# Banded attention and two MoE layers on one core: a new order of ScalarE's and VectorE's work in each attention step

## The chip, the cores and the metric

The kernel runs on one core of a Trainium2 chip. The metric is device time in microseconds (us) of one launch, the median over runs: 1203.46 us before the change (three runs, 1202.03 to 1204.03).

## What is computed

Attention with 4 batches, 8 heads, 768 positions and 64 channels, with a causal band of 96 positions and 8 global columns, then two feed-forward blocks over the 3072 tokens, all in float32:

```python
scores = scale * np.matmul(q, k.transpose(0, 1, 3, 2)) + bias     # bias: -slope * distance
scores = np.where(keep, scores, -1000000000.0)
scores = scores - np.max(scores, axis=-1, keepdims=True)
a = np.exp(scores)
a = a / (np.sum(a, axis=-1, keepdims=True) + 1e-09)
x = np.matmul(a, v)                       # 4 x 8 x 768 x 64, turned into 3072 x 512
h = x @ w_in                              # 512 -> 2048
x = (h * np.clip(h + 3.0, 0.0, 6.0) / 6.0) @ w_out
out = ((x @ w1) * (x @ w2) @ w3) @ w_out2 # 512 -> 1024 -> 1024 -> 512
```

## The kernel before

**Split products.** Most matrix products are made from two parts of each operand: a high part, which ScalarE rounds from the value, and a low part, the value minus the high part, which VectorE or GpSimd subtracts. `split_ps` (L353 to L364) does this for a tile in PSUM: ScalarE's copy (L357) makes the high part `...h`, and the closure `low` makes the low part `...l` on VectorE (L360). With a list as `later` the closure is only appended, and its instruction is issued where the list is run. `mm3` (L66) issues the three products high-high, low-high, high-low.

**Units and steps.** Attention is cut into 32 units (batch, half of the positions, pair of heads) of three steps each; a step `s` is one block of 128 queries for two heads. The loop at L608 is a software pipeline written by hand; each engine works through its instructions in the order in which this loop issues them:

- Every second step (a pair step) TensorE computes the products with v of two earlier steps (`a_pv`, tile `pv`, one PSUM buffer), then the scores of two new steps (`a_scores`, tiles `s0`, `s1`).
- In the first step of a unit `prep_k` transposes the next unit's k (`pk`), in the second `prep_q` its q (`pq`). ScalarE makes `kh` (three copies) or `qh`. From unit 8 on the scores take split operands, and the low parts `kl` (three, L360) or `ql` (L392) go to the list `lows`. Units below 8 have no low parts here (ScalarE's copy is then L355).
- `a_trans` transposes the weights of two steps ago (`pt`), `a_copy` brings them to SBUF on ScalarE (`p`, L461). `pk`, `pq` and `pt` share two PSUM buffers.
- `a_norm` makes the reciprocal of the row sums `su` on VectorE (L444, L445) and multiplies `e` by it on GpSimd (L446). `a_max` adds the bias and takes the row maxima on VectorE (L429, two per step), `a_exp` the exponentials on ScalarE (L438).
- `a_out` splits the products with v (`pv`) into `xt0h`/`xt0l` or `xt1h`/`xt1l`, the input of the first feed-forward layer.
- `tick` advances the conversion of the feed-forward weights, which come as float64: ScalarE makes `cva` (L158) from the loaded tile `st`, VectorE joins the bits in `cvt` (L171, L173, L175), ScalarE rounds `wa` (L184), and VectorE (for the first weights) or GpSimd makes its low part (L185). A step has one to four ticks, four while the weights of the first products are awaited (L605).
- `fill.run` puts matmuls of the feed-forward layer of an earlier block (`h`, `x`, L66) with their gates (L513 on ScalarE, L514 on VectorE, L497 and L500 for the parts `g`) between these. The first filler is added after step 14.

In a step VectorE's order before is: the reciprocal, the low parts of the products with v, the maxima, conversions and gates, and the low parts in `lows` after `a_exp`, with two conversions' places ahead of them where there are four ticks. ScalarE's is: `kh` or `qh`, the high parts of the products with v, conversions and gates, `p`, the exponentials.

Of the kernel before, what the change touches and what calls it, by code (L numbers as in the profile page):

```python
# [74 lines left out]
def kernel(ctx: ExitStack, tc: tile.TileContext, q, k, v, n_global, n_local,  # L75
# [104 lines left out]
    def awaited(*kinds):  # L180
        return any(key is not None and key[0] in kinds for key in queued)
# [40 lines left out]
    def tick(n=1):  # L222
        for _ in range(n):
            next(ticks)
            ticked[0] += 1
# [122 lines left out]
    def new_prep(i):  # L348
        def two(tag, shape):
            return tuple(att.tile(shape, F32R, tag=tag + z, name=tag + z) for z in "hl")  # L350
        prep[i] = dict(q=two("q", [P, HB * P]), k=two("k", [P, 2 * HB, P]))

    def split_ps(hi, lo, src, later=None, whole=False):  # L353
        if whole:
            nc.scalar.activation(hi.bitcast(F32), src, AF.Copy)  # L355
            return
        nc.scalar.activation(hi, src, AF.Copy)  # L357

        def low():
            nc.vector.tensor_tensor(lo, src, hi.bitcast(F32), ALU.subtract)  # L360
        if later is None:
            low()
        else:
            later.append(low)  # L364

    def prep_k(i, later):
        hf = units[i][1]
        nk = HB + hf
        kr = raw[i][0].rearrange("p n j d -> p n (j d)")
        ps = psa.tile([P, HB + 1, P], F32, tag="pt", bufs=2, name="pk")  # L370
        for s in range(nk):
            nc.tensor.transpose(ps[:, s, :], kr[:, s, :], ident)  # L372
        own, gp = (0, 1) if hf == 0 else (1, 0)
        ng = HB - 1 + hf
        kh, kl = (x.rearrange("p (n s) c -> p n s c", s=2) for x in prep[i]["k"])
        split_ps(kh[:, :, own], kl[:, :, own], ps[:, hf:hf + HB], later, i < WHOLE)
        split_ps(kh[:, :ng, gp, GW:], kl[:, :ng, gp, GW:], ps[:, 0:ng, GW:], later, i < WHOLE)
        src = ps[:, 0:1, 0:GW].to_broadcast([P, ng, GW])
        split_ps(kh[:, :ng, gp, 0:GW], kl[:, :ng, gp, 0:GW], src, later, i < WHOLE)

    def prep_q(i, later):
        b, hf, hp = units[i]
        qr = raw[i][1].rearrange("p n j d -> p n (j d)")
        ps = psa.tile([P, 512], F32, tag="pt", bufs=2, name="pq")
        for s in range(HB):
            nc.tensor.transpose(ps[:, s * P:(s + 1) * P], qr[:, s, :], ident)
        qh, ql = prep[i]["q"]
        src = ps[:, 0:HB * P]
        sc = qsc[:, hp:hp + 1]
        nc.scalar.activation(qh.bitcast(F32) if i < WHOLE else qh, src, AF.Copy, scale=sc)  # L390
        if i >= WHOLE:
            later.append(lambda: nc.vector.scalar_tensor_tensor(ql, src, sc, qh.bitcast(F32), ALU.mult, ALU.subtract))  # L392
# [4 lines left out]
    def kidx(hf, u):  # L397
        if hf:
            return 2 * u, 2
        return (0, 1) if u == 0 else (2 * u - 1, 2)  # L400

    def a_scores(sts):

        sc = [psa.tile([P, 2, 2 * P], F32, tag=f"s{j}", name=f"s{j}") for j in range(2)]
        for half, st in enumerate(sts):
            i, u = st
            b, hf, hp = units[i]
            c0, nk = kidx(hf, u)
            W = nk * P
            qq, kk = prep[i]["q"], prep[i]["k"]  # L410
            passes = ((0, 0),) if i < WHOLE else ((0, 0), (1, 0), (0, 1))
            for z, (a, b_) in enumerate(passes):
                for j in range(2):
                    r0 = D * j
                    x = qq[a][r0:r0 + D, u * P:(u + 1) * P]
                    y = kk[b_][r0:r0 + D, c0:c0 + nk, :].rearrange("p a c -> p (a c)")
                    if i < WHOLE:
                        x, y = x.bitcast(F32), y.bitcast(F32)
                    nc.tensor.matmul(sc[j][:, half, :W], x, y, start=(z == 0), stop=(z == len(passes) - 1))  # L419
            sm[st] = dict(sc=[x[:, half] for x in sc], W=W, nk=nk, c0=c0, hp=hp)  # L420

    def a_max(st):
        d = sm[st]
        W, hp = d["W"], d["hp"]
        e = att.tile([P, 2, 2 * P], F32, tag="e", name="e", bufs=3)
        mx = att.tile([P, 2], F32, tag="mx", name="mx", bufs=3)
        bs = base0 if d["nk"] == 1 else base1
        for j in range(2):
            nc.vector.tensor_tensor_reduce(e[:, j, :W], d["sc"][j][:, :W], bs, -slope[2 * hp + j], 3.0e38,  # L429
                                           ALU.add, ALU.min, mx[:, j:j + 1])  # L430
        d["e"], d["mx"] = e, mx
# [9 lines left out]
    def a_norm(st):  # L441
        d = sm[st]
        W, su = d["W"], d["su"]
        nc.vector.tensor_scalar(su, su, 1.0e-9, None, ALU.add)  # L444
        nc.vector.reciprocal(su, su)  # L445
        nc.gpsimd.tensor_tensor(d["e"][:, :, :W], d["e"][:, :, :W], su.unsqueeze(2).to_broadcast([P, 2, W]), ALU.mult)  # L446

    def a_trans(st):
        d = sm[st]
        nk = d["nk"]  # L450
        ps = psa.tile([P, 2, 2, P], F32, tag="pt", bufs=2, name="pt")
        for j in range(2):
            for t in range(nk):
                nc.tensor.transpose(ps[:, t, j, :], d["e"][:, j, t * P:(t + 1) * P], ident)  # L454
        d["pt"] = ps

    def a_copy(st):
        d = sm[st]
        nk = d["nk"]
        d["p"] = att.tile([P, 2, 2, P], F32, tag="p", name="p", bufs=4)  # L460
        nc.scalar.activation(d["p"][:, :nk], d["pt"][:, :nk], AF.Copy)  # L461

    def a_pv(sts):

        ps = psa.tile([P, 2, P], F32, tag="pv", name="pv")
        for half, st in enumerate(sts):
            i, u = st
            d = sm[st]
            nk, c0 = d["nk"], d["c0"]
            for t in range(nk):  # L470
                for j in range(2):
                    nc.tensor.matmul(ps[D * j:D * j + D, half], raw[i][2][:, c0 + t, j, :], d["p"][:, t, j, :],  # L472
                                     start=(t == 0), stop=(t == nk - 1))
        sm[sts[0]]["pv"] = ps

    def a_out(sts):
        ps = sm[sts[0]]["pv"]
        runs = [(0, 2)] if sts[0][0] == sts[1][0] else [(0, 1), (1, 2)]
        low = []
        for h0, h1 in runs:  # L480
            i, u = sts[h0]
            b, hf, hp = units[i]
            xh, xl = xT[(2 * b + hf) % 2]
            cs = slice(u * P, (u + h1 - h0) * P)
            split_ps(xh[:, hp, cs], xl[:, hp, cs], ps[:, h0:h1].rearrange("p a q -> p (a q)"), low)
        for f in low:
            f()
        for st in sts:
            sm.pop(st)

# [83 lines left out]
    with tc.tile_pool(name="mk", bufs=1) as mk:  # L574
        base = masks(mk)
        next(base)
        for prep_x in (prep_k, prep_q):
            lows = []
# [26 lines left out]
    def nticks(s):  # L605
        return 1 if s < 4 else 4 if awaited("wi", "wo") else 2

    for s in range(NS + 3):  # L608
        lows = []
        more = s < NS and steps[s][0] + 1 < NU  # L610
        now = [steps[s - d] if 0 <= s - d < NS else None for d in range(3)]
        pair = steps[s - 4:s - 2] if s % 2 == 0 and 4 <= s < NS + 4 else None
        u = now[0][1] if now[0] else None
        i = now[0][0] if now[0] else None
        if pair:
            a_pv(pair)
        if now[0] and s % 2 == 0:
            a_scores(steps[s:s + 2])
        if more:
            if u == 0:  # L620
                new_prep(i + 1)
                prep_k(i + 1, lows)
            elif u == 1:
                prep_q(i + 1, lows)
        if now[2]:
            a_trans(now[2])
        if now[1]:
            a_norm(now[1])
        if pair:
            a_out(pair)  # L630
        if now[0]:
            a_max(now[0])
        n = nticks(s)
        if n > 1:
            tick()
        fill.run(slot / 4)
        if now[2]:
            a_copy(now[2])
        if n > 2:
            tick()  # L640
        if now[0]:
            a_exp(now[0])
        for f in lows:
            f()
        lows = []
        fill.run(slot / 4)
        if n > 3:
            tick()
        fill.run(slot / 4)
        if n > 0:  # L650
            tick()
        if more and u == 2:
            load_unit(i + 3)
        fill.run(slot / 4)
        if s >= 3 and (s - 2) % per == 0:
            fill.drain(pump)
            fill.add(gen_a((s - 3) // per))
# [562 lines left out]
```

## Time and profile before

| | |
|---|---|
| median of three runs | 1203.46 us (1202.03 to 1204.03) |
| the profiled execution, its own time | 1203.56 us |
| its span, first to last instruction | 1201.8 us |
| TensorE busy | 1144.0 us (95%) |
| VectorE, ScalarE, GpSimd busy | 684.6, 535.5, 433.9 us |
| TensorE's mean granted clock | 0.983 of full speed |

The span is divided into stretches by time from its start. Attention fills the first 445 us or so: up to 26 us loads and set-up, up to about 105 us the first units while the first weights are converted, then attention with filler matmuls in it. The second feed-forward block takes the last 380 us. Busy times say how full an engine is; what an engine waits for is read from its idle time and from the timeline.

### The profile page before, as it was taken

Reading aid. Unit: us, or ns where it says so; the run is one execution under the profiler, and the core shown is the slowest. Engines: PE = TensorE matmul, PEld = TensorE weight load, DVE = VectorE, ACT = ScalarE, POOL = GpSimd, SP = SyncE. Lnnn points to the kernel's source line nnn. Section 1 sums busy time; section 2 is a strip of 40 time slices with the busy share of each in tenths; the row PEclk is TensorE's granted clock in tenths of the full one; section 3 lists DMA queues with packets and bytes.
Section 4 is the critical chain, followed back from the end, with each engine's and each line's share of the span. In section 5 each row is a group of like instructions: output and inputs, shape, how many; then the busy total and the mean of one; then the engine's idle time right before and its main releaser. Section 6 shows DMA issues by size and latency. Waiting matters only on the chain.

```text
span 1201.8 us, 19626 instructions
## 1 busy us (share of the span) xinstructions
PE 1144.0 (95%) x7040; PEld 1063.7 (89%) x7040; DVE 684.6 (57%) x1495; ACT 535.5 (45%) x1282; POOL 433.9 (36%) x370
## 2 busy tenths in 40 slices
PE   5699999999999999999899999999999999999995
PEld 3478898999898999999799999899899899899894
DVE  4888766576666424264554433446584573675662
ACT  4787667676767645444333232441332312231210
POOL 2134334242423322255321123774452421543620
PEclk9799999999999999999999999999999999999998
DMA  7775867676674104444844437416203155224112
GB/s 166 191 219 147 225 173 205 177 211 192 165 203 129 42 27 147 150 160 165 280 137 147 172 117 254 152 34 219 93 13 105 54 197 205 74 85 158 54 51 91
DMA packets 190187, 173.90 MB, mean 145 GB/s; under 512 B 111232, under 2 KB 151168, under 8 KB 190080
## 3 DMA queue, kind: packets, MB, share of 16 engines
q1 hardware_dynamic: 189792, 172.54, 46.8%
q8 instruction: 58, 0.95, 0.3%
q14 instruction: 49, 0.40, 0.1%
q10 hardware_dynamic: 288, 0.00, 0.0%
HBM read 116.92 MB, written 55.57 MB: 144 GB/s over the span
## 4 chain that ended last, share of the span: by engine, by line
PE 81%; DVE 6%; DMA 4%; ACT 3%; SPq 2%; issue 2%; POOL 1%; POOLq 0%; DVEq 0%; ACTq 0%
PE b L66 30%; PE x L66 19%; PE h L66 17%; PE wo L66 3%; PE pv L472 3%; PE s L419 3%; PE pt L454 3%; SPq L259 1%; DMA st<-in_moe_w_dram 1%; PE pk L372 1%; POOL wa L185 1%; DVE e L429 1%; DVE kl L360 1%; DVE cvt L175 1%; DVE cvt L173 1%
## 5 line engine op out<-in xcount | busy, mean ns | idle before, releaser
L66 PE MATMUL b<-x,wa 128*128 128x384 f32 x960 | 173.3, 339 | 0.7 <-DVE part L833 0.7
L66 PEld LDWEIGHTS b<-x,wa 128*128 128x128 f32 x960 | 169.6, 188 | 1.7 <-issue 1.0
L446 POOL TENSOR_TENSOR e<-e,su 128x512 f32<-128x512 f32 (+1 forms) x96 | 93.0, 969 | 212.1 <-DVE su L445 187.1
L902 DVE TENSOR_TENSOR u<-b,u 128x768 f32<-128x768 f32 x112 | 105.2, 951 | 102.9 <-PE b L66 90.0
L514 DVE SCALAR_TENSOR_TENSOR t<-t,h 128x384 f32<-128x384 f32 x128 | 70.6, 552 | 132.8 <-ACT t L513 132.6
L438 ACT ACTIVATE e<-e,mx 128x256 f32<-128x256 f32 (+1 forms) x192 | 93.0, 492 | 20.8 <-DVE mx L429 20.3
L513 ACT ACTIVATE t<-h,c 128x384 f32<-128x384 f32 x128 | 73.7, 576 | 56.4 <-PE h L66 56.3
L158 ACT ACTIVATE cva<-st 128x512 f32<-128x512 f32 x72 | 48.1, 668 | 57.3 <-DMA st<-in_moe_w_dram 27.5
L429 DVE CUSTOM_DVE_ANT_0 e<-s,base 128x256 f32<-128x256 f32 (+1 forms) x192 | 69.1, 398 | 2.2 <-PE s L419 1.9
L454 PE MATMUL pt<-ident,e 128*128 128x128 f32 x352 | 58.7, 288 | 10.6 <-DVE kl L360 7.4
L472 PE MATMUL pv<-p,rv 128*64 128x128 f32 x704 | 52.6, 286 | 16.5 <-ACT p L461 16.5
L175 DVE SCALAR_TENSOR_TENSOR cvt<-cva,cvt 128x512 uint32<-128x512 uint32 x72 | 67.6, 940 | 1.0
L66 PE MATMUL h<-xt0h,wa 128*128 128x384 f32 x256 | 67.9, 341 | 0.0
L66 PE MATMUL h<-xt1h,wa 128*128 128x384 f32 x256 | 67.2, 339 | 0.0
L461 ACT ACTIVATE p<-pt 128x512 f32<-128x512 f32 (+1 forms) x96 | 54.9, 571 | 25.3 <-PE pt L454 25.2
L472 PEld LDWEIGHTS pv<-p,rv 128*64 128x64 f32 x704 | 38.3, 139 | 30.8 <-ACT p L461 19.2
L500 POOL TENSOR_TENSOR g0l<-t,g0h 128x384 fp32r<-128x384 f32 x16 | 17.5, 1096 | 128.6 <-ACT g0h L497 128.6
L897 DVE TENSOR_TENSOR u<-u 128x384 f32<-128x384 f32 x64 | 62.2, 972 | 1.6
L185 POOL TENSOR_TENSOR wa<-st,wa 128x512 fp32r<-128x512 f32 x32 | 43.2, 1358 | 46.0 <-ACT wa L184 31.7
L454 PEld LDWEIGHTS pt<-ident,e 128*128 128x128 f32 x352 | 42.0, 146 | 18.5 <-issue 14.7
L173 DVE SCALAR_TENSOR_TENSOR cvt<-st,cvt 128x512 uint32<-128x512 uint32 x72 | 57.7, 801 | 0.9
L500 POOL TENSOR_TENSOR g3l<-u,g3h 128x384 fp32r<-128x384 f32 x8 | 8.1, 1018 | 135.0 <-ACT g3h L497 123.5
(435 smaller groups left out, 3110.7 us busy)
## 6 DMA issues: line engine op xcount, KB each, us to landing
st<-in_moe_w_dram SPq DMA_DIRECT2D x32, 512.0 KB, 5.5
st<-in_moe_w_out_dram SPq DMA_DIRECT2D x24, 512.0 KB, 4.2
st<-in_moe_w_in_dram SPq DMA_DIRECT2D x16, 512.0 KB, 4.3
wb<-cvt SPq DMA_DIRECT2D x32, 256.0 KB, 2.3
st<-wb SPq DMA_DIRECT2D x32, 256.0 KB, 2.9
wt<-wa SPq DMA_DIRECT2D x32, 256.0 KB, 3.3
wa<-wt SPq DMA_DIRECT2D x32, 256.0 KB, 5.4
rk<-in_k_dram SPq DMA_DIRECT2D x64, 96.0 KB, 4.3
```

Source lines behind the costliest of these rows:

```text
L66: nc.tensor.matmul(out, a, b, start=(first and i == 0 and j == 0), stop=(last and i == n - 1 and j == 2))
L173: nc.vector.scalar_tensor_tensor(tu, low, 29, tu, ALU.logical_shift_right, ALU.bitwise_or)
L175: nc.vector.scalar_tensor_tensor(tu, au, 0x80000000, tu, ALU.bitwise_and, ALU.bitwise_or)
L429: nc.vector.tensor_tensor_reduce(e[:, j, :W], d["sc"][j][:, :W], bs, -slope[2 * hp + j], 3.0e38, ALU.add, ALU.min, mx[:, j:j + 1])
L438: nc.scalar.activation(e[:, j, :W], e[:, j, :W], AF.Exp, bias=mx[:, j:j + 1], scale=-1.0, accum_out=su[:, j:j + 1])
L446: nc.gpsimd.tensor_tensor(d["e"][:, :, :W], d["e"][:, :, :W], su.unsqueeze(2).to_broadcast([P, 2, W]), ALU.mult)
L454: nc.tensor.transpose(ps[:, t, j, :], d["e"][:, j, t * P:(t + 1) * P], ident)
L472: nc.tensor.matmul(ps[D * j:D * j + D, half], raw[i][2][:, c0 + t, j, :], d["p"][:, t, j, :], start=(t == 0), stop=(t == nk - 1))
L513: nc.scalar.activation(t, h, AF.Relu, bias=c3)
L514: nc.vector.scalar_tensor_tensor(t, t, 6.0, h, ALU.min, ALU.mult)
L897: nc.vector.tensor_tensor(x[:, 0], x[:, 0], x[:, 1], ALU.mult)
L902: nc.vector.tensor_tensor(o, x[:, :, :NA], y, ALU.add)
```

## The change

`a_out` no longer runs its low parts; it hands them to `lows`, and it is issued ahead of `prep_k`/`prep_q`. The list `lows`, with the low parts of the products with v first and those of k or q behind them, runs right after `a_max` and ahead of the first conversion of the step.

```diff
-    def a_out(sts):
+    def a_out(sts, low):
         ps = sm[sts[0]]["pv"]
         runs = [(0, 2)] if sts[0][0] == sts[1][0] else [(0, 1), (1, 2)]
-        low = []
         for h0, h1 in runs:
...
             split_ps(xh[:, hp, cs], xl[:, hp, cs], ps[:, h0:h1].rearrange("p a q -> p (a q)"), low)
-        for f in low:
-            f()
         for st in sts:
             sm.pop(st)
...
         if now[0] and s % 2 == 0:
             a_scores(steps[s:s + 2])
+        if pair:
+            a_out(pair, lows)
         if more:
             if u == 0:
                 new_prep(i + 1)
...
         if now[1]:
             a_norm(now[1])
-        if pair:
-            a_out(pair)
         if now[0]:
             a_max(now[0])
+        for f in lows:
+            f()
         n = nticks(s)
         if n > 1:
             tick()
...
         if now[0]:
             a_exp(now[0])
-        for f in lows:
-            f()
-        lows = []
         fill.run(slot / 4)
```

No instruction is added or removed; `lows` is emptied at the start of each step as before. TensorE's order and the order of the DMAs keep their places.

ScalarE, a pair step in an early unit (`kh` is the high part of k, `xt0h` that of the products with v, `wa_83` a converted weight), before:

```order
28 L158 ACTIVATE cva<-st 128x512
29 L355 ACTIVATE kh<-pk 128x3x128
30 L355 ACTIVATE kh<-pk 128x2x96
31 L355 ACTIVATE kh<-pk 128x2x32
32 L357 ACTIVATE xt0h<-pv 128x128 x2
33 L184 ACTIVATE wa_83<-cvt 128x512
```

and the difference at that place:

```order
+L357 ACTIVATE xt0h<-pv 128x128 x2
 L355 ACTIVATE kh<-pk 128x3x128
 L355 ACTIVATE kh<-pk 128x2x96
 L355 ACTIVATE kh<-pk 128x2x32
-L357 ACTIVATE xt0h<-pv 128x128 x2
 L184 ACTIVATE wa_83<-cvt 128x512
```

The two copies out of `pv` stand ahead of the three of k, and the weight's copy L184 follows those of k directly.

VectorE, a pair step in a later unit, in which low parts of k are due (`su` row sums, `e,mx` the maxima), before:

```order
434 L444 TENSOR_SCALAR su<-su 128x2
435 L445 RECIPROCAL su<-su 128x2
436 L360 TENSOR_TENSOR xt1l<-pv,xt1h 128x128 x2
437 L429 ISA e,mx<-s_2650,base_156 128x256
438 L429 ISA mx 128x1
439 L429 ISA e,mx<-s_2651,base_156 128x256
440 L429 ISA mx 128x1
441 L171 TENSOR_SCALAR cvt<-cva 128x512
442 L514 SCALAR_TENSOR_TENSOR t<-t,h 128x384
443 L360 TENSOR_TENSOR kl<-pk,kh 128x3x128
444 L360 TENSOR_TENSOR kl<-pk,kh 128x3x96
445 L360 TENSOR_TENSOR kl<-pk,kh 128x3x32
```

and after:

```order
434 L444 TENSOR_SCALAR su<-su 128x2
435 L445 RECIPROCAL su<-su 128x2
436 L429 ISA e,mx<-s_2650,base_156 128x256
437 L429 ISA mx 128x1
438 L429 ISA e,mx<-s_2651,base_156 128x256
439 L429 ISA mx 128x1
440 L360 TENSOR_TENSOR xt1l<-pv,xt1h 128x128 x2
441 L360 TENSOR_TENSOR kl<-pk,kh 128x3x128
442 L360 TENSOR_TENSOR kl<-pk,kh 128x3x96
443 L360 TENSOR_TENSOR kl<-pk,kh 128x3x32
444 L171 TENSOR_SCALAR cvt<-cva 128x512
445 L511 SCALAR_TENSOR_TENSOR t<-t,h 128x384
```

The maxima have moved ahead of the low parts of the products with v, and the three low parts of k ahead of the conversion L171 and the gate (L514 before, L511 in the changed file).

## Rows read from the trace of the kernel before

**Rows 1.** The page, part 1: engine, busy us (share of span), instructions.

```profile
PE 1144.0 (95%) x7040; PEld 1063.7 (89%) x7040; DVE 684.6 (57%) x1495; ACT 535.5 (45%) x1282; POOL 433.9 (36%) x370
```

**Rows 2.** Busy us of the engines by stretch: start:end, length, busy (instructions), clock, DMA.

```profile
26.00:62.00 36.00, 23.26 (x142) 15.62 (x142) 29.12 (x87) 27.29 (x81) 7.46 (x8) 0.69 0.78 206
62.00:105.00 43.00, 39.14 (x278) 33.83 (x279) 39.59 (x103) 34.92 (x94) 17.98 (x17) 0.97 0.67 189
105.00:450.00 345.00, 338.50 (x2655) 314.48 (x2654) 211.68 (x730) 227.97 (x669) 123.16 (x123) 1.00 0.58 159
450.00:560.00 110.00, 110.00 (x628) 110.00 (x627) 49.91 (x78) 50.69 (x92) 41.16 (x36) 1.00 0.45 151
560.00:620.00 60.00, 54.06 (x299) 50.73 (x298) 31.80 (x51) 23.56 (x45) 23.89 (x21) 1.00 0.59 204
```

**Rows 3.** TensorE's waits, 70 to 110 us, then 110 to 450: us, times, longest.

```profile
PE pt L454 <- DVE kl L360: 1.0, 1, 1.0
...
PE pt L454 <- DVE kl L360: 6.4, 8, 1.1
```

**Rows 4.** VectorE's waits, 26 to 105 us.

```profile
DVE xt0l L360 <- ACT xt0h L357: 5.2, 3, 2.5
...
DVE wa L185 <- ACT wa L184: 1.2, 1, 1.2
DVE xt1l L360 <- ACT xt1h L357: 0.9, 2, 0.5
```

**Rows 5.** Timeline of an early pair step: start us, us, engine, line, operation [idle before].

```profile
27.77 1.66 PE L419 MATMUL s<-kh,qh 64*128 64x128 f32 x8
...
28.84 0.17 DVE L445 RECIPROCAL su<-su 128x2 f32<-128x2 f32 x1
29.18 1.04 POOL L446 TENSOR_TENSOR e<-e,su 128x512 f32<-128x512 f32 x1 [4.42 <-DVE su L445]
...
30.29 0.83 ACT L355 ACTIVATE kh<-pk 128x384 f32<-128x384 f32 x3 [1.66 <-PE pk L372]
...
30.99 0.47 ACT L357 ACTIVATE xt0h<-pv 128x128 fp32r<-128x128 f32 x2
...
31.30 0.66 ACT L184 ACTIVATE wa<-cvt 128x512 fp32r<-128x512 f32 x1
31.49 0.49 DVE L360 TENSOR_TENSOR xt0l<-pv,xt0h 128x128 fp32r<-128x128 f32 x2 [2.48 <-ACT xt0h L357]
...
32.31 0.69 DVE L185 TENSOR_TENSOR wa<-cvt,wa 128x512 fp32r<-128x512 f32 x1
```

**Rows 6.** Timeline of a later pair step, with filler matmuls left out.

```profile
193.14 0.17 DVE L445 RECIPROCAL su<-su 128x2 f32<-128x2 f32 x1
...
193.87 0.93 ACT L357 ACTIVATE kh<-pk 128x384 fp32r<-128x384 f32 x3 [0.86 <-PE pk L372]
...
195.17 0.49 DVE L360 TENSOR_TENSOR xt1l<-pv,xt1h 128x128 fp32r<-128x128 f32 x2 [1.86 <-ACT xt1h L357]
...
195.58 0.41 DVE L429 CUSTOM_DVE_ANT_0 e<-s,base 128x256 f32<-128x256 f32 x1
...
197.31 1.07 DVE L360 TENSOR_TENSOR kl<-pk,kh 128x384 fp32r<-128x384 f32 x3
...
198.53 0.63 PE L454 MATMUL pt<-ident,e 128*128 128x128 f32 x4 [1.13 <-DVE kl L360]
```

**Rows 7.** Timeline at 60 us: GpSimd's multiplication and VectorE's L185 beside it.

```profile
60.42 1.04 POOL L446 TENSOR_TENSOR e<-e,su 128x512 f32<-128x512 f32 x1 [4.63 <-DVE su L445]
...
60.89 1.11 DVE L185 TENSOR_TENSOR wa<-cvt,wa 128x512 fp32r<-128x512 f32 x1
```

**Rows 8.** VectorE's groups by line, 26 to 62 us, then 105 to 450: busy, mean ns.

```profile
L175 DVE SCALAR_TENSOR_TENSOR cvt<-cva,cvt 128x512 uint32<-128x512 uint32 x8 | 5.5, 692 | 0.3
...
L175 DVE SCALAR_TENSOR_TENSOR cvt<-cva,cvt 128x512 uint32<-128x512 uint32 x31 | 33.8, 1089 | 0.0
```

**Rows 9.** The chain that ended last, at 573 us.

```profile
573.40 7.03 DMA st<-in_moe_w_dram
```

## The prediction
> **What bounds the kernel now.** The first view is the busy time of each engine [rows 1]: TensorE is busy 95% of the span, VectorE 57%, ScalarE 45%. An order of VectorE's and ScalarE's work can only matter where TensorE waits, so the next view is the busy time by stretch [rows 2]. The reader is to see four regimes. From 26 to 62 us TensorE is busy 23.26 of 36 us while VectorE has 29.12 and ScalarE 27.29: attention without filler, in which engines hand work to each other and none is full. From 62 to 105 us VectorE is the fullest, 39.59 of 43 us. From 105 to 450 us TensorE is busy 338.50 of 345 us and VectorE only 211.68 (61%): TensorE is the bound, and its idle 6.5 us are all that a better order could give there. From 450 us on no instruction is moved.
>
> The third view is what each engine waits for. TensorE's waits from 110 to 450 us are one line: the transposes `pt` wait for VectorE's `kl`, 8 times, 6.4 us, and once more just before, 1.0 us [rows 3]. That is the whole idle time of the stretch. VectorE's waits from 26 to 105 us are led by its low parts of the products with v, which wait for ScalarE's high parts: 5.2 us in three, and 0.9 us in two later ones [rows 4]. The timelines show how both come about, below.
>
> **Part 1, the first units (26 to 105 us).** In the step of [rows 5] VectorE is done with its reciprocal at 28.84 + 0.17 = 29.01 and then stands still for 2.48 us, because its next instruction in order is `xt0l`. That needs `xt0h`, which ScalarE issues behind `kh`; and `kh` waits for the transposes of k, which TensorE makes behind the scores. The maxima stand behind `xt0l` though the scores end at 27.77 + 1.66 = 29.43. The conversion L185 starts at 32.31.
>
> After the change the maxima run from about 29.4, the two low parts behind them (0.49 us, and their high parts now run ahead of `kh`, in ScalarE's 1.66 us of idle time). Both are over before 31 us. VectorE's next instruction is L185, which needs ScalarE's L184. L184 now follows `kh` directly: it starts at 30.99, where `xt0h` started, not at 31.30, and ends about 30.99 + 0.66 = 31.65. So L185 starts at 31.65 and not at 32.31: 0.66 us of the 2.48 come back, and the rest of the wait goes over to L184. This is the price of one such wait: what is late next is a copy that is only 0.31 us earlier. The second and third of the three waits are shorter (5.2 - 2.48 = 2.7 together), and the same argument holds in them, with the work of maxima and low parts, 0.7 to 1.2 us, taken out of the way of L185. I take 0.8 us for each of the three, 2.4 us. The bounds are 0 (another wait, a load of weights, paces the conversions) and 6.1 us (all five waits vanish whole, 5.2 + 0.9). I take a value far from the upper end because the row at 31.30 shows what takes over; the two late waits of 0.9 us I leave to the range.
>
> **Part 2, TensorE's stalls (103 to 450 us).** In the step of [rows 6] TensorE would have started the transposes at 198.53 - 1.13 = 197.40; the PSUM buffer that they write is that of `pk`, and it is free when the three `kl` are done, 197.31 + 1.07 = 198.38. `kl` is so late because it stands behind `xt1l` (which waits 1.86 us for ScalarE), the maxima, a conversion and a gate. After the change: reciprocal done at 193.31, two maxima (0.41 us each, to about 194.15), the two low parts of the products with v (0.49, to 194.65; their high parts are made before `kh`), then `kl`, which needs the last `kh`, 193.87 + 0.93 = 194.80. So `kl` runs from 194.8 to 195.9, 2.5 us earlier than before and 1.5 us ahead of TensorE's need. The longest stall is 1.13 us, so all nine go: 6.4 + 1.0 = 7.4 us. What is late next there is nothing that the waits show, as no other line of TensorE's stands in the list; a hidden one may cost, and as lower bound I take half, 3.7 us. The upper bound is 7.4, since TensorE has no other idle time.
>
> **Part 3, what is moved later.** The low parts of the products with v leave `pv` later by two maxima, 0.8 us; `pv` is next written two steps on, and the 96 steps of attention take over 4 us each (some 420 us for all of them): nothing. The conversions of a step with `kl` come 1.07 us later, and VectorE may stand at `kl` until `kh` is done, with the conversion L171 and a gate queued behind. The gate needs ScalarE's copy L513, which stands behind `kh` on ScalarE in both orders, so it loses nothing by that; the conversion's cover is VectorE's free time, 345 - 211.68 = 133 us, against 24 times 1.07 us = 26 us (units 8 to 31). If the cover were gone, the weights of the later products would come up to 26 us later, but they are not needed until after attention. ScalarE's high parts move forward into a wait [rows 5, 6], which delays nothing: `kh` has its idle time in front of it, 1.66 and 0.86 us. SP's and GpSimd's queues keep their order.
>
> **What conversions lose beside GpSimd.** Rows show that a conversion can take longer: L185 took 1.11 us at 60.89, begun while GpSimd's multiplication of 60.42 to 61.46 ran [rows 7], against 0.69 us [rows 5]; L175 has a mean of 692 ns before 62 us and of 1089 ns from 105 to 450 us [rows 8]. The Trainium skill, "SBUF — State Buffer", section "Who interferes with whom", says that a VectorE instruction with two inputs in SBUF and a GpSimd one that reads SBUF exclude each other, the second waiting in full, while one with a single SBUF input is not touched; the trace agrees for L185 (0.57 us of hold, then 0.54 us of work). By that rule an order that puts the PSUM readers (maxima, low parts) right behind the reciprocal, when GpSimd's multiplication starts, and conversions later loses nothing in these steps; the moved conversions may instead meet GpSimd's other subtractions, and that is the third rival.
>
> **Sum.** 1203.56 (the profiled execution; 1.76 us of it lie outside the span and stay) - 2.4 - 7.4 = 1193.8 us. That execution stands 0.1 us over the median of the runs, so I put 1193.7.
>
> **Rivals.**
> 1. The start gains nothing, because loaded weights pace it: the DMA engines are busy 0.78 from 26 to 62 us [rows 2]. Against it: the loads are issued when a converted tile is free, so they move with VectorE. It would give 1203.56 - 7.4 = 1196.2.
> 2. The gain is partly given back behind attention. From 450 to 560 us TensorE is busy throughout, but from 560 to 620 us it idles 60 - 54.06 = 5.9 us [rows 2], and there a load of 7.03 us lies on the chain [rows 9]. For it: a load that does not come earlier with TensorE would eat the gain as a longer wait. Against it: these loads are issued behind instructions in the same order. With half given back, 1203.5 - 4.9 = 1198.6; with all, 1203.5.
> 3. Slower: the conversions moved behind `kl` and `ql` meet GpSimd's subtractions of the gate's low parts, whichever comes second waits, and TensorE waits for a late `g` part. One L175 or L173 of 0.69 us [rows 8] is the hold. There are 48 steps with `kl` or `ql`; it decides when over 9.8 / 0.69 = 14 of them pass their hold on to TensorE. With half of them, 24 x 0.69 = 16.6 us, less the 9.8: 1210.3. For it: 1089 ns shows that holds are common. Against it: TensorE has not one wait for GpSimd in that stretch, though L175 is held there already.
> 4. The change does not do what it says: TensorE's stalls only change their name, because `pq`, which shares the buffers, or the next `pt` waits for `kl` or for ScalarE's `p` just as long. Then 1203.5. Against it: `p` is not made later by anything here.
>
> **How the numbers follow.** The forecast has 0.62, rival 1 has 0.15, rival 2 has 0.12, rival 3 has 0.05, rival 4 has 0.06. A measurement here can tell about 0.2% (2.4 us) from no change. Faster by more than that: the forecast, rival 1 and half of rival 2, 0.83. Within it: rival 4 and the other half of rival 2, 0.12. Slower: 0.05. The range: downward the upper bound of the start in the main with the stalls gone, 7.4 + 5.9 = 13.3, 1190.3; upward to take in rivals 1 and the larger part of 2, 1201.5. What is left out is rivals 3, 4 and a rest, under 0.2.
>
> **What would show it.** Right: TensorE's wait for `kl` from 103 to 450 us gone from its waits, and its busy time in that stretch equal to its length; VectorE's waits for `xt0h` in the first 105 us gone, with a shorter wait at L185 for L184 in their place; the filler's solid stretch, from about 445 us, beginning 8 to 11 us earlier, and the distance from there to the end unchanged. Part 1 is wrong if TensorE reaches the first filler matmuls at the same time as before; part 2 if another line stands in TensorE's waits with 4 us or more; part 3 if TensorE waits for GpSimd's `g` parts or if the stretch at 560 us has more idle time than 5.9 us.

## The result, and the profile after

The changed kernel takes 1190.93 us (median of four runs, 1189.93 to 1191.35), the kernel before beside it 1203.74 us (1202.03 to 1205.48): a ratio of 0.9893 [0.9878, 0.9909], faster by 12.8 us of these medians. Forecast were 1193.7 us and, against the profiled execution of before, -9.8 us; the time lies inside the range, near its lower end. The profiled execution of the changed kernel took 1191.16 us, with a span of 1189.3 us against 1201.8.

The busy times, page part 1, answer to [rows 1]: the engines do the same work, and VectorE and GpSimd need a little less time for it.

```profile
PE 1142.7 (96%) x7040; PEld 1064.7 (90%) x7040; DVE 678.7 (57%) x1495; ACT 535.4 (45%) x1282; POOL 431.4 (36%) x370
```

**Where the time came from.** The start of the score matmuls (L419) of a pair step can be read to 0.01 us in the timeline and marks the same place of the program in both kernels. Three of them for the changed kernel, the first score matmuls of the 4th, the 12th and the 48th pair step (start, duration, engine, line, operation):

```profile
28.04 1.66 PE L419 MATMUL s<-kh,qh 64*128 64x128 f32 x8
...
99.84 1.13 PE L419 MATMUL s<-kh,qh 64*128 64x256 f32 x8
...
418.78 0.39 PE L419 MATMUL s<-kh,qh 64*128 64x256 f32 x2
```

and the latter two for the kernel before, whose 4th stands in [rows 5] at 27.77:

```profile
101.37 1.13 PE L419 MATMUL s<-kh,qh 64*128 64x256 f32 x8
...
429.78 0.39 PE L419 MATMUL s<-kh,qh 64*128 64x256 f32 x2
```

Each kernel was profiled three times in all (the two repeats of each are among the experiments). With the 13th pair step (111.22 us before, 108.89 after, the first with split operands in its scores) as a fourth mark, the means of three are:

| from the start of | before | changed | gain |
|---|---|---|---|
| the span, to the 4th pair step | 27.54 | 28.14 | -0.60 |
| the 4th, to the 12th (first units) | 73.92 | 71.44 | 2.48 |
| the 12th, to the 13th | 9.84 | 9.05 | 0.79 |
| the 13th, to the 48th (units with split operands) | 318.57 | 309.89 | 8.67 |
| the 48th, to the end | 772.14 | 770.91 | 1.23 |
| sum, the mean span | 1202.0 | 1189.43 | 12.57 |

The stretch from the 13th to the 48th repeats to 0.02 us among the three profiles of a kernel; the first units spread by up to 0.6 us, the last row by up to 0.9. So three quarters of the gain (0.79 + 8.67 = 9.46 us) lie between the 12th and the 48th pair step, where TensorE is the bound. TensorE's clock is no rival for the first units: from the 4th to the 12th pair step the granted clock was 0.84, 0.80 and 0.83 of full speed in the mean before (a mix of its two levels, 1.2 and 2.4 GHz) and 0.84, 0.83 and 0.85 in the changed kernel, and at 0.84 the two took 73.60 and 71.80 us, at 0.83 73.99 and 71.29.

The busy time by stretch of the changed kernel, with the columns of [rows 2] (the third stretch ends 10 us sooner, as attention does; the last two lie 11.7 us sooner than before, by which the changed kernel is ahead there, so that they hold the same work):

```profile
26.00:62.00 36.00, 25.66 (x150) 17.23 (x151) 30.60 (x89) 28.20 (x82) 7.46 (x8) 0.69 0.80 210
62.00:105.00 43.00, 39.89 (x284) 35.18 (x283) 40.21 (x106) 34.93 (x94) 18.77 (x17) 0.97 0.71 197
105.00:440.00 335.00, 335.00 (x2647) 313.41 (x2646) 204.76 (x724) 226.93 (x665) 119.91 (x122) 1.00 0.59 163
438.30:548.30 110.00, 110.00 (x628) 110.00 (x627) 49.25 (x76) 50.52 (x92) 40.72 (x35) 1.00 0.46 151
548.30:608.30 60.00, 55.10 (x298) 52.12 (x297) 30.98 (x52) 22.99 (x44) 24.25 (x20) 0.97 0.58 198
```

The reader is to see that TensorE is busy 335.00 of 335 us in the third row. The first row alone shows little: 25.66 of 36 us, in the repeats 23.75 and 25.15, against 23.26, 24.21 and 23.40 before. In the last row TensorE idles 60 - 55.10 = 4.9 us; before it was 5.9 here and 60 - 54.96 = 5.0 in a repeat, so the idle time there has not changed beyond its spread.

VectorE's waits from 26 to 105 us answer to [rows 4]:

```profile
DVE wa L185 <- ACT wa L184: 3.9, 4, 1.5
DVE cvt L171 <- ACT cva L158: 3.6, 1, 3.6
DVE e L429 <- PE s L419: 0.9, 2, 0.6
DVE t L511 <- ACT t L510: 0.6, 1, 0.6
```

No low part of the products with v waits any more; 6.1 us of such waits are gone, and 2.7 us more stand at L185, which waits for ScalarE's L184. The wait of 3.6 us at L171 (2.6 before) is one for a load, and lies ahead of the 4th pair step; it comes up again below. The early step of [rows 5], in the timeline of the changed kernel:

```profile
28.04 1.66 PE L419 MATMUL s<-kh,qh 64*128 64x128 f32 x8
...
28.81 0.43 ACT L357 ACTIVATE xt0h<-pv 128x128 fp32r<-128x128 f32 x2
...
29.12 0.17 DVE L445 RECIPROCAL su<-su 128x2 f32<-128x2 f32 x1
...
29.84 0.29 DVE L429 CUSTOM_DVE_ANT_0 e<-s,base 128x128 f32<-128x128 f32 x1 [0.55 <-PE s L419]
...
30.27 0.48 DVE L360 TENSOR_TENSOR xt0l<-pv,xt0h 128x128 fp32r<-128x128 f32 x2
...
30.56 0.83 ACT L355 ACTIVATE kh<-pk 128x384 f32<-128x384 f32 x3 [1.32 <-PE pk L372]
...
31.26 0.64 ACT L184 ACTIVATE wa<-cvt 128x512 fp32r<-128x512 f32 x1
...
31.94 0.69 DVE L185 TENSOR_TENSOR wa<-cvt,wa 128x512 fp32r<-128x512 f32 x1 [1.19 <-ACT wa L184]
```

`xt0h` now runs while ScalarE would have waited for the transposes of k, the low parts run behind the maxima, and L185 waits 1.19 us for L184. It starts 31.94 - 28.04 = 3.90 us behind the scores' start; before it was 4.54, and the prediction's 31.65 is 3.88.

And the later step of [rows 6], with filler and two maxima's second halves left out:

```profile
189.20 0.42 DVE L429 CUSTOM_DVE_ANT_0 e<-s,base 128x256 f32<-128x256 f32 x1 [0.81 <-PE s L419]
...
189.89 0.48 DVE L360 TENSOR_TENSOR xt1l<-pv,xt1h 128x128 fp32r<-128x128 f32 x2
...
190.64 1.09 DVE L360 TENSOR_TENSOR kl<-pk,kh 128x384 fp32r<-128x384 f32 x3 [0.27 <-ACT kh L357]
191.65 0.75 DVE L171 TENSOR_SCALAR cvt<-cva 128x512 uint32<-128x512 uint32 x1
...
193.04 0.60 PE L454 MATMUL pt<-ident,e 128*128 128x128 f32 x4
```

`kl` is done at 190.64 + 1.09 = 191.73, and the transposes `pt` start at 193.04 without a wait, 1.3 us later (forecast: 1.5). The maxima wait 0.81 us for the scores, which the prediction had not seen coming; it costs nothing, since `kl` would have waited for `kh` in any case.

### The profile page after: what moved, and what is told of

The parts are those of the page before. It is cut to its first block, busy times and chain, and to the rows that moved or that the text cites. A ratio compares the mean times of both kernels' runs of the same rounds, so it can differ in the third digit from the quotient of the medians.

```text
span 1189.3 us, 19625 instructions
## 1 busy us (share of the span) xinstructions
PE 1142.7 (96%) x7040; PEld 1064.7 (90%) x7040; DVE 678.7 (57%) x1495; ACT 535.4 (45%) x1282; POOL 431.4 (36%) x370
## 4 chain that ended last, share of the span: by engine, by line
PE 83%; DMA 5%; DVE 4%; SPq 2%; issue 2%; POOL 2%; ACT 2%; POOLq 0%; DVEq 0%; ACTq 0%
PE b L66 30%; PE x L66 19%; PE h L66 19%; PE wo L66 3%; PE pv L472 3%; PE s L419 3%; PE pt L454 3%; DMA st<-in_moe_w_dram 1%; PE pk L372 1%; SPq L259 1%; PE pq L386 1%; POOL wa L185 1%; DVE cvt L173 1%; DVE cvt L175 1%; PE wt L734 1%
## 5 line engine op out<-in xcount | busy, mean ns | idle before, releaser
L446 POOL TENSOR_TENSOR e<-e,su 128x512 f32<-128x512 f32 (+1 forms) x96 | 93.0, 969 | 201.8 <-DVE su L445 165.9
L511 DVE SCALAR_TENSOR_TENSOR t<-t,h 128x384 f32<-128x384 f32 x128 | 70.7, 552 | 137.4 <-ACT t L510 137.4
L158 ACT ACTIVATE cva<-st 128x512 f32<-128x512 f32 x72 | 48.3, 671 | 56.3 <-DMA st<-in_moe_w_dram 30.4
L175 DVE SCALAR_TENSOR_TENSOR cvt<-cva,cvt 128x512 uint32<-128x512 uint32 x72 | 61.7, 856 | 1.1
L497 POOL TENSOR_TENSOR g0l<-t,g0h 128x384 fp32r<-128x384 f32 x16 | 17.4, 1089 | 123.5 <-ACT g0h L494 123.5
L185 POOL TENSOR_TENSOR wa<-st,wa 128x512 fp32r<-128x512 f32 x32 | 43.3, 1360 | 43.3 <-ACT wa L184 34.9
L173 DVE SCALAR_TENSOR_TENSOR cvt<-st,cvt 128x512 uint32<-128x512 uint32 x72 | 55.1, 766 | 1.3
```

The costliest lines, as they stand in the source:

```text
L173: nc.vector.scalar_tensor_tensor(tu, low, 29, tu, ALU.logical_shift_right, ALU.bitwise_or)
L175: nc.vector.scalar_tensor_tensor(tu, au, 0x80000000, tu, ALU.bitwise_and, ALU.bitwise_or)
L511: nc.vector.scalar_tensor_tensor(t, t, 6.0, h, ALU.min, ALU.mult)
```

## The experiments

Two theories were set against each other first. **Theory 1**, that of the prediction: ScalarE's order holds VectorE in the first units, and low parts of k that come late stall TensorE behind them. **Theory 2**: the gain comes from the maxima, hence the exponentials and `p`, being earlier. The change was taken apart into three pieces, and one kernel joins two of them.

**ScalarE's order alone** (against the kernel before): the high parts of the products with v ahead of `kh` and `qh`; VectorE's order as before.

```diff
         if now[0] and s % 2 == 0:
             a_scores(steps[s:s + 2])
+        outs = []
+        if pair:
+            a_out(pair, outs)
...
-        if pair:
-            a_out(pair)
+        for f in outs:
+            f()
         if now[0]:
             a_max(now[0])
```

> Only ScalarE's order is changed (high parts of the products with v ahead of those of k or q); VectorE keeps the order of before. Theory 1 (ScalarE's order holds VectorE in the first units; the late place of the low parts of k stalls TensorE later): the start gains all that it gained with the whole change (scores near 100 us reached about 1.5 to 2 us earlier), and since the low parts of the products with v no longer wait, the low parts of k come some 1.5 us earlier and the stalls fall from 7.4 to under 1.5 us: 1192 to 1195 us. Theory 2 (what counts is that the maxima, and so the exponentials and p, come ahead of the low parts): less than half of the gain, 1197 to 1203 us.

Measured: 1193.48 us (1192.7 to 1193.59) against 1203.29 (1201.3 to 1204.95), 0.9918 [0.9905, 0.9932].

**The maxima first, alone**: they go ahead of the low parts of the products with v, on VectorE only.

```diff
+        outs = []
         if pair:
-            a_out(pair)
+            a_out(pair, outs)
         if now[0]:
             a_max(now[0])
+        for f in outs:
+            f()
```

> Only the maxima are put ahead of the low parts of the products with v on VectorE; ScalarE's order and the place of the low parts of k and q are those of before. Theory 1: the start gains 0.3 to 1 us (VectorE still waits for the high parts behind those of k, with only the maxima out of the way), the low parts of k come about 0.5 us earlier, so the stalls fall to 1.5 to 4 us: 1196 to 1200 us. Theory 2: nearly the whole gain, 1190 to 1193 us.

Measured: 1197.37 us, 0.9951 [0.9937, 0.9964].

**The low parts of k and q early, alone**: right behind the maxima, ahead of the conversions.

```diff
         if now[0]:
             a_max(now[0])
+        for f in lows:
+            f()
         n = nticks(s)
...
         if now[0]:
             a_exp(now[0])
-        for f in lows:
-            f()
-        lows = []
```

> Only the low parts of k and q are moved ahead of the conversions, right behind the maxima; the products with v are handled as before. Theory 1: the start is unchanged; the low parts of k end about 1.0 us earlier, so nearly all stalls go (under 1 us left), and each costs a little more than its idle time shows: 1194 to 1197 us. Theory 2: no change, 1202 to 1204 us.

Measured: 1196.9 us, 0.9947 [0.9933, 0.996]. The time is as theory 1 has it; of the stalls 1.76 us are left (the marks below), where under 1 us was expected.

**All but the maxima**: the first and the third edit together, so that only the place of the maxima differs from the changed kernel.

> The whole change without the maxima ahead of the low parts of the products with v: ScalarE's order and the early place of the low parts of k and q. Theory 1: as the changed kernel, 1190 to 1192.5 us. Theory 2: at least 4 us slower than the changed kernel, 1195 us or more.

Measured: 1191.4 us (1190.73 to 1192.55), 0.9905 [0.989, 0.992], beside the changed kernel's 1190.93.

The marks of the four tell the places apart (us; one profile each, beside the means above):

| | 4th to 12th | 12th to 13th | 13th to 48th |
|---|---|---|---|
| before | 73.92 | 9.84 | 318.57 |
| ScalarE's order | 71.43 | 9.86 | 310.53 |
| maxima first | 73.64 | 9.85 | 312.56 |
| low parts of k, q early | 74.51 | 9.05 | 311.65 |
| all but the maxima | 70.6 | 9.06 | 309.89 |
| changed | 71.44 | 9.05 | 309.89 |

Only the kernels with ScalarE's new order gain in the first units; the maxima alone gain nothing there that the spread would show. That spread is 0.9 us: the kernel with the low parts of k and q early has the order of before on every engine up to 99.6 us, and took 74.51 us where the kernel before took 73.60 to 74.16. VectorE's waits for the high parts from 26 to 105 us fit: 1.2 us with ScalarE's order,

```profile
DVE xt0l L360 <- ACT xt0h L357: 1.2, 2, 0.7
```

3.5 us with the maxima first,

```profile
DVE xt0l L360 <- ACT xt0h L357: 3.5, 3, 1.4
```

and 6.3 us with the low parts of k and q early. In the later units each piece alone takes most of the 8.67 us (8.0, 6.0 and 6.9), far more together than there is. That is what a stall with a bounded size does: `kl` has to come earlier only by as much as TensorE waits, 1.3 us at most (the weight loads' row further below), and any of the three gives most of that. All but the maxima reach the full 309.89, so the place of the maxima is worth nothing beside the other two. Theory 1 holds, theory 2 falls.

The step from the 12th to the 13th gains only where the low parts of k and q are early, and less than its stall: of 1.2 us before the loads of weights for `pt`, in the kernel before,

```profile
PEld pt L454 <- issue: 1.2, 1, 1.2
```

a part comes back in the changed kernel as a wait for GpSimd's `e`, so 0.79 us are gained:

```profile
PEld pt L454 <- POOL e L446: 0.5, 1, 0.5
```

**What paces the first units now.** Theory A says VectorE's work does; theory B says TensorE's wait for `p`, which ScalarE makes too late, does. TensorE's list of waits of the changed kernel, 26 to 105 us, seems to speak for B:

```profile
PE pv L472 <- ACT p L461: 15.1, 8, 5.3
```

First the changed kernel again, as a reference beside the next three:

> The changed kernel once more, beside the next three. If the 1.5 us that the part behind attention gained is chance, its length from the 48th scores to the end falls anywhere from 770.5 to 772.5 us, and from the 13th to the 48th scores it is again 309.9 us; if the change itself shortens the part behind, its length is again 770.5 us. Total 1190 to 1192 us.

Measured: 1191.22 us (1189.94 to 1194.49) against 1205.4 (1203.73 to 1207.38), 0.9889 [0.9874, 0.9905].

**`p` early** (against the changed kernel): the copies `p` go ahead of the step's conversions and filler.

```diff
         for f in lows:
             f()
+        if now[2]:
+            a_copy(now[2])
         n = nticks(s)
...
         fill.run(slot / 4)
-        if now[2]:
-            a_copy(now[2])
```

> The changed kernel, with ScalarE's copy of p ahead of the step's first conversion and filler. Theory A (VectorE's conversions bound the first 105 us, where it is busy 70.8 of 79 us): little, 1189 to 1192 us. Theory B (TensorE's 15 us of waits for p there are the bound): 3 to 6 us faster than the changed kernel, 1185 to 1188 us. From the 13th to the 48th scores nothing changes, 309.9 us, as TensorE has no wait left.

Measured: 1193.52 us (1193.11 to 1194.26), 0.9903 [0.9888, 0.9918], 2.3 us more than the reference and above what either theory gave. The first units do not gain (71.22 us from the 4th to the 12th pair step, 71.29 in the reference); the step from the 12th to the 13th is longer, 10.28 against 9.06, and what follows the 48th too, 772.89 against 770.82, for which nothing here gives a cause. Behind the earlier `p` stands what ScalarE makes later: VectorE's wait for L184 has grown from 3.5 us in the reference to

```profile
DVE wa L185 <- ACT wa L184: 5.2, 4, 1.8
```

TensorE's waits from 26 to 105 us, in the reference

```profile
PE pv L472 <- ACT p L461: 13.3, 6, 4.2
PE pt L454 <- POOL e L446: 1.7, 3, 1.1
```

and with `p` early

```profile
PE pv L472 <- ACT p L461: 10.9, 6, 4.4
PE pt L454 <- POOL e L446: 4.5, 5, 1.4
```

show that 2.4 us of the wait for `p` went and 2.8 us came as waits for `e`. So ScalarE's place for `p` is not the lever, and in this form theory B falls; 10.9 us of waits for `p` are left, whose causes this kernel did not touch.

**The first weights' low parts on GpSimd** (against the changed kernel): the 16 subtractions L185 of these weights leave VectorE for GpSimd.

```diff
-    first_weights = ("wi", "wo", "wib", "wob")
+    first_weights = ("wib", "wob")
```

> The changed kernel, with the low parts of the first layer's first weights (L185, some 16 in the first 105 us, 0.7 to 1.1 us each) on GpSimd in place of VectorE. Theory A: VectorE loses about 14 us of work in the first 105 us, of which the next limit gives back a part: 1181 to 1187 us. Theory B: within 1.5 us of the changed kernel, or slower (to 1196 us) where the row sums' multiplication queues behind the subtractions on GpSimd (1.36 us each).

Measured: 1192.87 us (1192.52 to 1193.77), 0.9895 [0.988, 0.991]: no gain over the reference, as theory B had it, and the first units take 73.16 us, 1.9 more. The groups by line show why. VectorE's conversions from 26 to 105 us in the changed kernel (line, engine, operation, shape, count; busy us, mean ns of one; idle before them):

```profile
L185 DVE TENSOR_TENSOR wa<-cvt,wa 128x512 fp32r<-128x512 f32 x16 | 14.1, 882 | 3.9 <-ACT wa L184 3.9
L173 DVE SCALAR_TENSOR_TENSOR cvt<-st,cvt 128x512 uint32<-128x512 uint32 x17 | 13.1, 772 | 0.5
L175 DVE SCALAR_TENSOR_TENSOR cvt<-cva,cvt 128x512 uint32<-128x512 uint32 x17 | 12.4, 731 | 0.5
L171 DVE TENSOR_SCALAR cvt<-cva 128x512 uint32<-128x512 uint32 x18 | 8.3, 462 | 3.6 <-ACT cva L158 3.6
```

and the same lines with L185 on GpSimd:

```profile
L173 DVE SCALAR_TENSOR_TENSOR cvt<-st,cvt 128x512 uint32<-128x512 uint32 x17 | 24.4, 1436 | 0.5
L185 POOL TENSOR_TENSOR wa<-cvt,wa 128x512 fp32r<-128x512 f32 x16 | 22.7, 1418 | 3.7 <-ACT wa L184 3.5
L175 DVE SCALAR_TENSOR_TENSOR cvt<-cva,cvt 128x512 uint32<-128x512 uint32 x17 | 15.1, 890 | 0.5
L171 DVE TENSOR_SCALAR cvt<-cva 128x512 uint32<-128x512 uint32 x17 | 11.5, 675 | 2.4 <-ACT cva L158 2.4
```

VectorE is rid of 14.1 us, but L173, L175 and L171 take 24.4 + 15.1 + 11.5 = 51.0 us instead of 33.8: 17.2 us more. The timeline shows one such meeting, GpSimd's subtraction and the conversion begun beside it, which lasts until the subtraction is over at 41.00 us and 0.55 us more (alone it takes 0.69):

```profile
39.57 1.43 POOL L185 TENSOR_TENSOR wa<-cvt,wa 128x512 fp32r<-128x512 f32 x1 [0.25 <-ACT wa L184]
...
39.91 1.64 DVE L173 SCALAR_TENSOR_TENSOR cvt<-st,cvt 128x512 uint32<-128x512 uint32 x1
```

The Trainium skill, "SBUF — State Buffer", section "Who interferes with whom", says that a VectorE instruction with two inputs in SBUF and a GpSimd one that reads SBUF exclude each other; the trace agrees, 1436 ns against 772. The prediction's addition that an instruction with a single input in SBUF is not touched does not hold here: L171, which reads `cva` alone, went from 462 to 675 ns, and one that began at 42.87 us beside GpSimd's L446 (42.72 to 43.76) took 1.17 us. The work only went from one engine's time into the other's hold, so VectorE was not relieved, and theory A was not tested by this kernel. What bounds the first units stays open.

**Both**:

> Both of the two edits before. Theory A: with VectorE relieved the wait for p counts, and the two add up or more: 2 to 4 us faster than with the low parts on GpSimd alone. Theory B: as with p early alone, within 1.5 us.

Measured: 1194.6 us (1193.76 to 1195.37), 0.9909 [0.9894, 0.9924], 1.1 us more than with `p` early alone, within what theory B gave. The losses roughly add, 2.3 + 1.7 = 4.0 against 3.4 us. No version beats the changed kernel.

**The kernels again.** Two more profiles of the kernel before and one of the changed kernel, to see which differences between single profiles repeat:

> The kernel before, profiled once more. If the length of the part behind attention (48th scores to the end) is set by the order of the instructions, it is again 772.0 us to 0.3; if it is chance from execution to execution, it differs by up to 1.5 us. The 13th to the 48th scores again take 318.6 us, and the 4th to the 13th, where loads take part, 83.4 us to 1.0.

> The kernel before, a third time: as the run before this one, to see whether two executions of one program agree behind attention to 0.3 us.

> The changed kernel, a third time: by order, the part behind attention is again 770.5 to 770.8 us; by chance, anywhere from 770.5 to 772.5. The 13th to the 48th scores 309.9 us, the 4th to the 13th 80.3 to 80.9 us.

Measured, one execution each: 1203.98, 1203.82 and 1191.62 us. The marks went into the table of means above. What repeats: all the gains of its middle three rows. Ahead of the 4th pair step the changed kernel is later each time (before 27.77, 27.23, 27.62; changed 28.04, 28.13, 28.25), but so is the kernel with the low parts of k and q early, 28.37, whose order up to there is that of before. What follows the 48th pair step is shorter in the mean by 1.23 us, with a spread inside a kernel of up to 0.9 us and 772.19 us in the kernel with all but the maxima.

## Why the prediction was right, and where its size was off

**Part 1, the first units: right.** Forecast 2.4 us, measured 2.48 from the 4th to the 12th pair step. Its mechanism stands in the timeline, 3.90 us from scores to L185 for a forecast 3.88; the wait for `xt0h` is gone and a shorter one for L184 has taken its place. The separate kernels show that ScalarE's order makes the gain. The 0.8 us for each of the three waits was chosen between bounds, so that the sum came out so close is partly luck.

**Part 2, TensorE's stalls: the mechanism right, the size too small.** Forecast 7.4 us (1.0 + 6.4), measured 0.79 + 8.67 = 9.46. The step that failed is "That is the whole idle time of the stretch", and with it "The upper bound is 7.4, since TensorE has no other idle time". It took the idle time from the matmuls' rows. The loading of weights shows more. In the waits of TensorE's weight loads from 112 to 450 us the kernel before has

```profile
PEld pt L454 <- issue: 9.0, 13, 1.3
```

where the matmuls show 6.4 us in 8 [rows 3]. The changed kernel, same view:

```profile
PEld pt L454 <- issue: 0.2, 1, 0.2
```

With ScalarE's order alone:

```profile
PEld pt L454 <- issue: 0.9, 4, 0.2
```

With the maxima first:

```profile
PEld pt L454 <- issue: 2.9, 7, 0.6
```

With the low parts of k and q early:

```profile
PEld pt L454 <- issue: 2.0, 7, 0.3
```

One wait of 0.2 us lies behind the 48th pair step in every one of the five. Without it these are 8.8 us in twelve, 0.7 in three, 2.7 in six and 1.8 in six. The length from the 13th to the 48th pair step, less the changed kernel's 309.89, is 8.67, 0.64, 2.67 and 1.76 us. The loads give the cost of the stalls to 0.2 us in all four, while the matmuls show 6.4, nothing, 1.1 and nothing. (From the 12th to the 13th, where another wait follows, 1.2 us before the loads and 1.0 before the matmuls were worth 0.79.) One stall by itself: in the kernel before, from the scores at 192.26 to the next pair's at 202.91 us lie 10.65 us, and 9.33 in the changed kernel, 1.32 more. The matmuls' row gives 1.13 us of idle time there [rows 6], the weight load's 1.34:

```profile
198.50 0.42 PEld L454 LDWEIGHTS pt<-ident,e 128*128 128x128 f32 x4 [1.34 <-issue]
```

So each stall was read about 0.2 us too short, and four of the twelve were not seen. The rows of matmuls overlap: just before that stall one of 0.33 us starts at 196.56 us and the next at 196.73, so a row reaches 0.16 us beyond the next one's start, and idle time counted from its end comes out shorter by about that. The Trainium skill, "Perfetto Trace Analysis", section "Tensor Engine Instruction (MATMUL, LD_WEIGHTS)", says that the profiler estimates where a TensorE instruction ends, from its size and a delay; the trace agrees in so far as the matmuls' rows show 2.3 us less than the 8.67 us that were lost.

**Part 3, what is moved later: right.** From 112 to 450 us the changed kernel's TensorE has no matmul wait at all, neither for GpSimd's `g` nor for `pv`. The conversions as a whole did not lose beside GpSimd either; L175 takes 916 ns in the mean from 105 to 450 us, where it took 1089 [rows 8]:

```profile
L175 DVE SCALAR_TENSOR_TENSOR cvt<-cva,cvt 128x512 uint32<-128x512 uint32 x31 | 28.4, 916 | 0.0
```

**Not in the sum.** 0.6 us are lost ahead of the 4th pair step and 1.2 us gained behind the 48th. Neither was forecast. The loss is the landing of a load of weights: ScalarE's L158 waits for it, and `p`, the products with v and the 4th scores follow. In twelve of the thirteen profiles these scores start 1.60 to 1.62 us behind L158 (1.35 in the other). In the kernel before, the changed one and the one with the low parts of k and q early it starts at

```profile
26.16 0.66 ACT L158 ACTIVATE cva<-st 128x512 f32<-128x512 f32 x1 [3.01 <-DMA st<-in_moe_w_in_dram]
26.43 0.66 ACT L158 ACTIVATE cva<-st 128x512 f32<-128x512 f32 x1 [4.09 <-DMA st<-in_moe_w_in_dram]
26.76 0.66 ACT L158 ACTIVATE cva<-st 128x512 f32<-128x512 f32 x1 [3.58 <-DMA st<-in_moe_w_in_dram]
```

and with `p` early, where L158 still stands ahead of that `p`, at 25.62. The load is issued at 21.5 us in all four. Why it lands later in the changed kernel's three profiles (L158 at 26.43, 26.78, 26.64, before 26.16, 25.61, 26.01) stays open; that the order of the change does it is not shown, since the third of these kernels has the order of before up to there. The gain behind the 48th is of the size of the spread there.

**The range.** Its lower end left 5.9 us for the start, without a source (the bound given for it was 6.1). The start took 2.48 of it, and part 2 went 2.1 us beyond what was called its upper bound; that the time still lies in the range, 0.6 us above its end, is partly luck.

**The rivals.** Rival 1, a start paced by the loads, falls from the 4th pair step on, where the first units gained 2.48 us; ahead of it a load does set the time. Rival 2, a gain given back behind attention, falls: what follows the 48th pair step got no longer, and the load of [rows 9] moved with the rest, by 11.7 us:

```profile
561.67 6.96 DMA st<-in_moe_w_dram
```

Rival 3, slower by conversions held beside GpSimd, falls by the 916 ns and by TensorE's empty list. Rival 4, a stall that changes its name, falls by the same list from 112 us on; in one step, from the 12th to the 13th, 0.5 us of a stall did come back as a wait for `e`, and at L185 the wait changed its name too, which was in the sum.

## What to carry to other kernels

In an engine that works in order, an instruction whose input is ready belongs ahead of one that waits for another engine's answer; here two high-part copies moved into ScalarE's wait, and low parts issued when TensorE needs them, took 1.1% off. Once the late result comes ahead of its need, further pieces of such a change bring nothing, so their single gains do not add. Read what TensorE loses from its weight loads' idle time and from the distance between the same matmuls of two kernels, and take the matmuls' idle time as a lower bound of the stall alone. What removing the stall brings can be less, where another wait stands behind it (0.79 us of 1.2 in one step here).

## What the runs showed of the hardware

The matmul rows hide stalls of TensorE: 8.8 us of idle time before the loads of weights stood as 6.4 us before the matmuls, and stalls of 0.2 to 0.3 us each did not show there at all, though the time they cost can be read from the marks (0.64 us in three, 1.76 us in six).

Work moved from VectorE to GpSimd can cost VectorE more than it carried away: 14.1 us went, 17.2 us came back as conversions that took up to 1.9 times as long (L173, 772 to 1436 ns), and GpSimd needed 22.7 us for what VectorE had done in 14.1.
